# DMA transposes of attention's exponentials issued one step sooner, the first output tile turned inside the last gate/up unit, and two value banks exchanged

## The chip, the core and the metric

The kernel runs on one core of one Trainium2 chip. The metric is the device time of one execution in microseconds; lower is better. The core's engines work side by side, each through its own queue in order: TensorE (PE, with its weight loads PEld), VectorE (DVE), ScalarE (ACT), GpSimd (POOL), and SyncE (SP), which in this kernel issues every DMA. Matmul results go to PSUM, here named as eight banks, `bank0` to `bank7`.

## The reference

A sequence of 2048 rows of width 576 goes through an attention with a memory over four segments and through a gated feed-forward block; a gate per row mixes the two.

```python
g = _sigmoid((x * gate_w).sum(-1, keepdims=True))
a = _A_ref(x, wq, wk, wv, wo, beta)      # 32 heads of 18, 4 segments of 512
b = (_silu(x @ w_gate) * (x @ w_up)) @ w_down   # 576 -> 4608 -> 576
return g * a + (1 - g) * b
```

Shortened: within a segment the mask adds -1e9 where the query's index is below the key's. For each segment

```python
logits = jnp.einsum("bhqd,bhkd->bhqk", qs, ks) * scale + mask
p = _softmax(logits, axis=-1)
a_dot = jnp.einsum("bhqk,bhkd->bhqd", p, vs)
num, den = phi(qs) @ M, phi(qs) @ z + 1e-6
outs.append(sig * (num / den) + (1.0 - sig) * a_dot)   # sig = sigmoid(beta) per head
M, z = M + phi(ks).T @ vs, z + phi(ks).sum()
```

and the outputs of all heads go through `wo`.

## The kernel before

Float32 accuracy is reached with pairs of rounded values: an operand is split into a high and a low part (ScalarE copies the high part, VectorE subtracts it: the helper `split`, lines 128 and 129), and three matmuls take the place of one.

**Phase one (0 to about 220 us): projections.** For each of four segments `qk` makes nine chains of queries and keys (14 matmuls of 512 columns each, line 151), and `v_step` makes eight steps of values and of the row gate (14 matmuls of 288 or 290 columns, same line). The chains of the first segment take the banks 0 to 4 in turn (`first_tile`), those of later segments 0, 1 and 2 (`chain_tile`). The steps of the values take the banks that the list in `v_tile` names, one after the other; its first eight entries are those of the first segment. A chain's bank is last read by VectorE in line 368 (`ph`), a value step's by line 388, or by line 390 for the steps of the second half, which hold the gate's column. In segments two to four, sums of keys and values (`upd_gen`) run in between in the banks 3 and 4 (`pair_tile`).

**Phase two (about 220 to 1650 us): feed-forward and attention interleaved.** There are 72 gate/up units (`seq`): two halves of the rows (`HALF`) by 36 column blocks. Each unit is seven products (`seven`, lines 998 and 1001) after Strassen's scheme, and each is followed by a `tick`, which calls `beat`: it first runs the functions that are due (a list `due`; `defer(k, fn)` puts fn at the k-th beat from now; `plan` holds offsets, to which one is added), then a down group or two, and then steps of attention, according to a credit. Every third unit, 16 down groups (`down_group`, line 851: 9 matmuls of 320 or 256 columns from three blocks `hs` and `ds`) are put into the list `groups`; line 856 adds their result into `ya`. At the end of each half the groups of the last three blocks are left; for the first half they run in a break of ten beats (`BREAK`), for the second in the output stage.

Attention is a generator, `att_gen`, whose steps `tau` run six to a unit `u` of two heads (64 units). Step t of a unit (t = 0 to 4) holds one bank of logits: `s_bank` (PE line 720, VectorE's row minimum line 726) at tau = t, `e_bank` (ScalarE's exponentials line 738, POOL's triangle line 746) one step later, `p_bank` three steps later (`PL`): VectorE rounds to float16 (line 752) and POOL makes the rest (line 753). `x_bank` (line 757) has SP transpose both halves by DMA into `pt`, `XL` steps after `s_bank`. It is the last thing that its step does. At the sixth step of the next unit `v_unit` (lines 768 and 769) multiplies the five transposed tiles of a unit with the values. `p` has 4 buffers, `pt` has 7. At tau = 1 to 3 of a unit SP also issues the loads of the next unit's `qst` and `kst` (line 804), in the sixth sometimes the values `v` (line 206). Between these, in the same queue of SP, stand the loads and stores of the units: `raw` (line 213), `rh` (246), `draw` (218), `dc` and `dw` (833, 838), `rr` and `rc` (241, 239), `wc` (705).

**Output stage (about 1650 to 1746 us).** When attention is done (`c_open`), the weights `wo` are loaded in six pieces and split (lines 888 to 892), and the first tiles of attention's result are loaded (`c_load`: `o` and the memory's part `me`, lines 897 and 901). `c_tr` adds the two on POOL (line 913), copies a piece (line 914), turns the tile on PE in five transposes (lines 917 and 919, into bank 5 or 6 and bank 7), and splits the result. The loop over n = 0 to 16 turns tile n, does `downs(k)` (k of the 16 groups that are left), then for tile n - 1 both column halves: 14 matmuls with `wo`, `downs(1)`, and the mixing on VectorE (lines 1129 and 1130).

Of the kernel before, what the change touches and what calls it, by code (L numbers as in the profile page):

```python
# [36 lines left out]
NB = 8 * NSEG  # L37
NST = 2
PL = 3
XL = 5  # L40
KEPT = 2
HALF = ((2, 3), (0, 1))
TICK = ((0.57, 1.0), (0.47, 1.0))
# [22 lines left out]
def gated_mix(ctx, tc, xT, xrest, wf, wfr, wfh, wd, wv, wo, beta, cmask, ident, bmask, out):  # L66
# [32 lines left out]
    def banks(*ids):  # L99
        turn = cycle(ids)  # L100
        return lambda shape=(P, L): ps.tile(list(shape), F32, name=f"bank{next(turn)}")
# [3 lines left out]
    pair_tile = banks(3, 4)  # L105
    first_tile = banks(0, 1, 2, 3, 4)
    lone_tile = banks(7)
    v_tile = banks(5, 6, 7, 3, 4, 5, 6, 7, *8 * (5, 6, 7))
    a_tile = banks(0)
    x_tile = banks(1)  # L110
    y_tile = banks(2)
# [15 lines left out]
    def split(hi, lo, src):  # L127
        nc.scalar.activation(hi, src, AF.Copy)  # L128
        nc.vector.tensor_sub(lo, src, f32(hi))  # L129
# [31 lines left out]
    def xs_split(xs, raw):  # L161
        nc.scalar.activation(xs, raw, AF.Copy)
        nc.vector.tensor_sub(xs[64:128], raw[64:128], f32(xs[64:128]))
# [40 lines left out]
    def v_fetch(k):  # L204
        VP[k] = ap.tile([P, 4, 8, 3, E], BF, name="v")
        nc.sync.dma_start(VP[k], vd[k // 4, k // 2 % 2][:, :, 8 * (k % 2):8 * (k % 2) + 8])
# [477 lines left out]
    with ExitStack() as st:  # L684
# [12 lines left out]
        def row_tile():  # L697
            return rw.tile([P, L], F32, name="row")
# [93 lines left out]
        def att_gen():  # L792
            N = 12 * NB

            def at(t):
                return 5 * (t // 6) + t % 6 if 0 <= t < N and t % 6 < 5 else None

            for tau in range(N + 10):
# [17 lines left out]
                if n == 5 and 1 <= u <= 2 * NB:  # L816
                    v_unit(u - 1)
                    if u % 4 == 1 and u // 4 + 1 < 4 * NSEG:
                        v_fetch(u // 4 + 1)
                z = at(tau - XL)  # L820
                if z is not None:
# [39 lines left out]
        wos, tiles = [], {}  # L861
# [49 lines left out]
        def c_tr(o, me):  # L911
            if me is not None:
                nc.gpsimd.tensor_add(o[:, 0:D], o[:, 0:D], me)
            nc.gpsimd.tensor_copy(o[:, 576:640], o[:, 512:576])
            ta = half_tile([P, 4, P])
            for k in range(4):
                nc.tensor.transpose(ta[:, k], o[:, P * k:P * k + P], idt)
            tb = lone_tile([P, P])
            nc.tensor.transpose(tb, o[:, 512:640], idt)
            oh = cps[0].tile([P, 4, P], F32R, name="oh")  # L920
            ol = cps[0].tile([P, 4, P], F32R, name="ol")
            os_ = cps[0].tile([P, P], F32R, name="os")
            split(oh, ol, ta)
            xs_split(os_, tb)
            r = []
            for k in range(4):
                r += [oh[:, k], ol[:, k], oh[:, k]]
            return r + [os_, os_]
# [30 lines left out]
        def feed(half, f):  # L959
            return [(f // CH, i, hf, hs, ds, yas[half], half) for i in range(8) for hf in range(2)]  # L960
# [32 lines left out]
        def seven(t, j, first=True):  # L993
# [6 lines left out]
                    n += 1  # L1000
            nc.tensor.matmul(t, rem[:, RPOS[j]], XR[j], start=False, stop=True, skip_group_check=True)  # L1001

        draw = {}
        for o, fn in start:
            defer(o - 7, fn)
        for pos, (half, f) in enumerate(seq):
            if f == 0:
                yas[half] = yp.tile([P, 8, D], F32, name="ya")
            q = f % CH
            nxt = seq[pos + 1] if pos + 1 < len(seq) else None  # L1010
            if q == 0 and f:
                groups += feed(half, f - 1)
            plan = []
            if nxt:
                plan += w_fetch(nxt[1]) if nxt[0] and nxt[1] < KEPT else w_make(*nxt)
                if nxt != (0, 1):
                    plan.append((1 if nxt[1] else 10, lambda f=nxt[1]: r_fetch(f)))
                for n, h in enumerate(BLOCKS.get(pos, ())):
                    plan += r_block(h, 4 * n)
                if f + 2 < FT:  # L1020
                    wraw_of[f + 2] = [None, None]
                    for u in range(2):
                        plan.append(((2, 5)[u] if f or not half else 5 + u, lambda u=u, f=f: wraw_of[f + 2].__setitem__(u, w_load(f + 2, u))))
            if pos == FT - 2:
                X2, XR2 = [[None, None] for _ in range(7)], [None] * 7
                plan += [(o + 8, fn) for o, fn in x_second(X2, XR2)]
            for o, fn in plan:
                defer(o + 1, fn)
            step = [0]

            def tick():
                k = step[0]
                step[0] += 1
                if k == 0:
                    while stores:
                        nc.sync.dma_start(*stores.pop(0))
                if half == 0:
                    if (q, k) in ((0, 3), (1, 3), (2, 2)):
                        draw[f] = d_load(f)
                    if (q, k) in ((1, 1), (1, 7), (2, 4)):  # L1040
                        g = f - 1 if k == 1 else f
                        ds[half, g] = d_split(g, draw.pop(g))
                elif (q, k) in ((1, 0), (1, 2), (2, 1)):
                    g = f - 1 if k == 0 else f
                    ds[half, g] = d_fetch(g)
                beat(k, half)

            ops, rem = wops.pop((half, f)), rhs[f % 2]
            hh = fp.tile([P, 2, L], F32R, name="hh")
            hl = fp.tile([P, 2, L], F32R, name="hl")  # L1050
            hs[half, f] = hh, hl
            a, y, xx = a_tile(), y_tile(), x_tile()
            p5, sg0, sg1 = (row_tile() for _ in range(3))
            seven(a, 0)
            nc.scalar.activation(xx, a, AF.Copy)  # L1055
            tick()
            seven(y, 1)
            nc.scalar.activation(p5, y, AF.Copy)
            tick()
            seven(a, 2, False)  # L1060
            y = y_tile()
            nc.vector.tensor_add(y, a, p5)
            tick()
            seven(xx, 3, False)
            nc.scalar.activation(sg0, xx, AF.Copy)  # L1065
            tick()
            seven(a, 4, False)
            xx = x_tile()
            nc.scalar.activation(xx, a, AF.Copy)  # L1069
            nc.vector.tensor_add(p5, a, p5)  # L1070
            tick()
            nc.scalar.activation(sg0, sg0, AF.Silu)  # L1072
            seven(y, 5, False)
            nc.scalar.activation(sg1, y, AF.Silu)
            exp_table()
            tick()
            tick()
            seven(xx, 6, False)
            nc.vector.tensor_mul(sg0, xx, sg0)
            nc.vector.tensor_mul(sg1, p5, sg1)  # L1080
            if q == CH - 1:
                defer(2, lambda t=(hh[:, 0], hl[:, 0], sg0): split(*t))
            else:
                split_by(2, hh[:, 0], hl[:, 0], sg0)
            split_by(3, hh[:, 1], hl[:, 1], sg1)
            tick()
            assert not groups
            if f == FT - 1:
                groups += feed(half, f)
                if half == 0:  # L1090
                    for n in range(BREAK):
                        beat(None if n > 1 else n)
                    XO, XR = X2, XR2
                    assert not groups
# [13 lines left out]
        def downs(k):  # L1108
            for _ in range(min(k, len(groups))):
                down_group(*groups.pop(0))  # L1110

        ffs = {n: f_load(n) for n in range(2)}
        for n in range(17):
            if n < 16:
                if n + 2 < 16:
                    tiles[n + 2] = c_load(n + 2)
                    ffs[n + 2] = f_load(n + 2)
                nxt = c_tr(*tiles.pop(n))
                downs(2 if n else 4)
            if n:  # L1120
                tt = order[n - 1]
                ff = ffs.pop(n - 1)
                for hf in range(2):
                    c = slice(288 * hf, 288 * hf + 288)
                    t = chain_tile()
                    products(t[:, :288], ops, w_mov(wos[hf], 288))
                    downs(1)
                    if hf == 0:
                        nc.vector.tensor_scalar_mul(ff, ff, g1[:, tt:tt + 1])
                    nc.vector.scalar_tensor_tensor(ff[:, c], t[:, :288], gg[:, tt:tt + 1], ff[:, c],  # L1130
                                                   op0=OP.mult, op1=OP.add)
                    if hf == 0 and sent:
                        nc.sync.dma_start(*sent.pop(0))
                    if n == 16:
                        nc.sync.dma_start(out[0, P * tt:P * tt + P, c], ff[:, c])
                if n < 16:
                    sent.append((out[0, P * tt:P * tt + P, :], ff))
            ops = nxt
# [54 lines left out]
```

## Time and profile before

| | us |
|---|---|
| three runs | 1742.91, 1745.12, 1744.81 |
| median | 1744.81 |
| the profiled execution | 1747.73 |
| its span, first to last instruction | 1746.0 |
| its mean granted clock of TensorE | 0.998 |

The profile is of one execution. Its page gives the busy time of each engine; a view by stage gives it for stretches of the span, where the numbers are: the stretch, its length, then for PE, PEld, DVE, ACT and POOL the busy time and in brackets the number of instructions, then the granted clock of TensorE (1.00 is full speed), the busy share of the DMA engines, and GB/s. The list of waits has, for who waited and whom for, the total, the number and the longest. A row of the timeline is: start, duration, engine, line, operation, output and inputs, shapes, the number of instructions that were merged, and in brackets the idle time of the engine before it and what ended it. Rows of SP (marked SPq) are issues of DMAs: their duration is that of the issue, not of the transfer. A row of the chain of waits is: start, duration, what.

### The profile page before, as it was taken

Reading aid. Unit: us, or ns where it says so; the run is one execution under the profiler, and the core shown is the slowest. Engines: PE = TensorE matmul, PEld = TensorE weight load, DVE = VectorE, ACT = ScalarE, POOL = GpSimd, SP = SyncE. Lnnn points to the kernel's source line nnn. Section 1 sums busy time; section 2 is a strip of 40 time slices with the busy share of each in tenths; the row PEclk is TensorE's granted clock in tenths of the full one; section 3 lists DMA queues with packets and bytes.
Section 4 is the critical chain, followed back from the end, with each engine's and each line's share of the span. In section 5 each row is a group of like instructions: output and inputs, shape, how many; then the busy total and the mean of one; then the engine's idle time right before and its main releaser. Section 6 shows DMA issues by size and latency. Waiting matters only on the chain.

```text
span 1746.0 us, 34931 instructions
## 1 busy us (share of the span) xinstructions
PE 1715.8 (98%) x11868; PEld 1483.9 (85%) x11868; DVE 1368.6 (78%) x3231; ACT 1093.6 (63%) x2198; POOL 936.3 (54%) x1194
## 2 busy tenths in 40 slices
PE   9999999999999999999999999999999999999999
PEld 7899978878888888887887788888888888888799
DVE  6567587989898889898989677787888777887655
ACT  7666575765676577667656755665666576656511
POOL 4434645656665656665666555555555555555221
PEclk9999999999999999999999999999999999999999
DMA  7654499998998888897979976777687668866544
GB/s 263 237 190 154 149 307 179 213 221 180 225 216 206 175 207 199 187 199 192 209 146 287 263 176 132 188 168 157 156 185 173 155 149 186 169 129 147 168 134 139
DMA packets 524003, 328.06 MB, mean 188 GB/s; under 512 B 411184, under 2 KB 460336, under 8 KB 523824
## 3 DMA queue, kind: packets, MB, share of 16 engines
q1 hardware_dynamic: 523824, 325.83, 76.6%
q8 instruction: 93, 1.52, 0.4%
q14 instruction: 86, 0.70, 0.1%
HBM read 165.76 MB, written 76.09 MB: 139 GB/s over the span
## 4 chain that ended last, share of the span: by engine, by line
PE 78%; ACT 8%; DVE 4%; DMA 3%; issue 3%; POOL 2%; SPq 1%; DVEq 0%; ACTq 0%; POOLq 0%
PE bank L998 29%; PE bank L851 25%; PE bank L151 10%; PE bank L1001 5%; PE bank L720 3%; PE bank L768 2%; ACT L1072 1%; PE bank L769 1%; ACT L991 1%; DMA pt<-p 1%; ACT pe L738 1%; PE bank L406 1%; POOL ws L256 1%; DVE hl L941 1%; PE bank L342 1%
## 5 line engine op out<-in xcount | busy, mean ns | idle before, releaser
L753 POOL TENSOR_TENSOR p<-pe,p 128x512 f16<-128x512 f32 x320 | 374.4, 1170 | 457.7 <-DVE p L752 438.2
L851 PE MATMUL bank<-dw,hh 128*128 128x320 f32 (+1 forms) x2304 | 491.2, 306 | 4.1 <-ACT hh L128 2.8
L851 PEld LDWEIGHTS bank<-dw,hh 128*128 128x128 f32 x2304 | 383.3, 191 | 15.6 <-ACT hh L128 3.1
L738 ACT ACTIVATE pe<-bank,mb 128x512 f32<-128x512 f32 (+3 forms) x512 | 246.2, 522 | 219.7 <-DVE mb L726 216.0
L851 PE MATMUL bank<-dw,hl 128*128 128x320 f32 (+1 forms) x1152 | 341.6, 297 | 0.2 <-DVE hl L129 0.2
L726 DVE CUSTOM_DVE_ANT_0 scr<-bank,cm 128x512 bf16<-128x512 f32 (+3 forms) x512 | 246.1, 481 | 7.4 <-PE bank L720 0.6
L851 PEld LDWEIGHTS bank<-dw,hl 128*128 128x128 f32 x1152 | 219.1, 190 | 0.4 <-DVE hl L129 0.4
L856 DVE TENSOR_TENSOR ya<-bank,ya 128x320 f32<-128x320 f32 x352 | 157.7, 452 | 78.7 <-PE bank L851 77.9
L1001 PE MATMUL bank<-xr,rh 128*128 128x512 f32 x504 | 196.3, 390 | 0.0
L746 POOL TENSOR_SCALAR_AFFINE_SELECT pe<-pe 128x256 f32<-128x256 f32 (+1 forms) x320 | 151.1, 473 | 31.2 <-ACT pe L738 21.6
L752 DVE CAST p<-pe 128x512 f16<-128x512 f32 x320 | 145.3, 454 | 2.3 <-DMA pt<-p 2.3
L256 POOL TENSOR_TENSOR ws<-raw 128x256 f32<-128x256 f32 x140 | 123.2, 880 | 15.8 <-DVE wo__22847 L263 4.1
L720 PE MATMUL bank<-kst,qst 108*128 108x512 bf16 (+3 forms) x512 | 125.4, 306 | 5.0 <-ACT pe L738 4.9
L1001 PEld LDWEIGHTS bank<-xr,rh 128*128 128x128 f32 x504 | 94.6, 188 | 20.5
L941 DVE TENSOR_TENSOR hl<-row,hh 128x512 fp32r<-128x512 f32 x120 | 101.4, 845 | 10.8 <-ACT hh L940 10.4
L1065 ACT ACTIVATE row<-bank 128x512 f32<-128x512 f32 x72 | 43.1, 598 | 93.6 <-PE bank L1001 93.5
L1070 DVE TENSOR_TENSOR row<-bank,row 128x512 f32<-128x512 f32 x72 | 49.6, 689 | 58.4 <-ACT bank L1069 58.2
L1072 ACT ACT_TABLE_LOAD x72 | 92.4, 1283 | 1.3
L991 ACT ACT_TABLE_LOAD x72 | 92.4, 1283 | 1.0
L768 PE MATMUL bank<-v,pt 128*128 128x57 bf16 x1280 | 77.0, 188 | 8.8 <-DMA pt<-p 5.7
L1055 ACT ACTIVATE bank<-bank 128x512 f32<-128x512 f32 x72 | 41.7, 579 | 67.0 <-PE bank L1001 66.9
L366 POOL TENSOR_TENSOR q<-qr,q 128x512 bf16<-128x512 f32 x36 | 44.5, 1235 | 72.7 <-ACT q L365 61.9
(2166 smaller groups left out, 4139.0 us busy)
## 6 DMA issues: line engine op xcount, KB each, us to landing
raw<-in_wf_dram SPq DMA_DIRECT2D x140, 256.0 KB
rh<-rc SPq DMA_DIRECT2D x72, 336.0 KB
dc<-dw SPq DMA_DIRECT2D x36, 576.0 KB
dw<-dc SPq DMA_DIRECT2D x36, 576.0 KB
stk<-q SPq DMA_DIRECT2D x32, 384.0 KB
draw<-in_wd_dram SPq DMA_DIRECT2D x36, 288.0 KB
rc<-rt SPq DMA_DIRECT2D x42, 224.0 KB
vd<-vps SPq DMA_DIRECT2D x8, 912.0 KB
```

What stands on the lines that cost most here:

```text
L151: nc.tensor.matmul(t, st[n], mv[n], start=(n == 0), stop=(n == 13))
L256: (nc.gpsimd.tensor_sub if sub else nc.gpsimd.tensor_add)(src[j], p(), q())
L720: nc.tensor.matmul(t[:, c:c + w], qs[:KR, pr, P * i:P * i + P], ks[:KR, pr, 0:w], start=True, stop=True)
L726: nc.vector.tensor_tensor_reduce(scr[:, :w], t[:, c:c + w], cm[:, L - w:L], -SCALE, 3.0e38, OP.add, OP.min, m[:, k:k + 1])
L738: nc.scalar.activation(pe[:, c:c + w], t[:, c:c + w], AF.Exp, bias=m[:, k:k + 1], scale=SCALE)
L746: nc.gpsimd.affine_select(d, d, pattern=pat, compare_op=OP.is_ge, fill=0.0, base=0, channel_multiplier=1)
L752: nc.vector.tensor_copy(p[:, 0], pe)
L753: nc.gpsimd.tensor_sub(p[:, 1], pe, p[:, 0])
L851: nc.tensor.matmul(t, p, q[:, cs], start=(n == 0), stop=(n == 3 * CH - 1))
L856: nc.vector.tensor_add(ya[:, i, cs], t, ya[:, i, cs])
L998: nc.tensor.matmul(t, w[:, p, z], x[z][:, q], start=first and n == 0, stop=False, skip_group_check=True)
L1001: nc.tensor.matmul(t, rem[:, RPOS[j]], XR[j], start=False, stop=True, skip_group_check=True)
```

## The change

Three things are changed. `XL` goes from 5 to 4, so that `x_bank` runs one step of attention sooner, at the end of the step before. In `v_tile`, the entries for the steps 3 and 4 of the first segment become the banks 4 and 0 (they were 3 and 4). And tile 0 of the output stage is turned (`c_tr`) in the last gate/up unit, at the fourth beat, between its fourth and fifth product; the loop takes it from the list `early`, and the down groups are dealt out otherwise: none for n = 0 (four before), none ahead of tile 0's products for n = 1 (two before), two from n = 2 on as before.

```diff
@@ -37,7 +37,7 @@
 PL = 3
-XL = 5
+XL = 4
@@ -105,7 +105,7 @@
-    v_tile = banks(5, 6, 7, 3, 4, 5, 6, 7, *8 * (5, 6, 7))
+    v_tile = banks(5, 6, 7, 4, 0, 5, 6, 7, *8 * (5, 6, 7))
@@ -1000,6 +1000,7 @@
+        early = []
         draw = {}
         for o, fn in start:
             defer(o - 7, fn)
@@ -1011,6 +1012,8 @@
             plan = []
+            if not nxt:
+                plan.append((3, lambda: early.append(c_tr(*tiles.pop(0)))))
             if nxt:
@@ -1115,8 +1118,8 @@
-                nxt = c_tr(*tiles.pop(n))
-                downs(2 if n else 4)
+                nxt = c_tr(*tiles.pop(n)) if n else early.pop()
+                downs(2 if n > 1 else 0)
             if n:
```

## The prediction

> **What bounds the kernel now.** The page and its table by stage come first: which engine has no room.
>
> ```profile
> PE 1715.8 (98%) x11868; PEld 1483.9 (85%) x11868; DVE 1368.6 (78%) x3231; ACT 1093.6 (63%) x2198; POOL 936.3 (54%) x1194
> ...
> 250.00:300.00 50.00, 46.52 (x338) 39.95 (x336) 39.78 (x96) 30.92 (x64) 29.18 (x41) 1.00 0.89 198
> 1650.00:1700.00 50.00, 46.78 (x344) 45.96 (x343) 27.20 (x53) 9.17 (x21) 12.37 (x15) 0.97 0.48 161
> ```
>
> TensorE is busy 1715.8 of 1746.0 us, so only some 30 us are open to any reordering. Of these 3.5 us are lost in 250 to 300 and 3.2 in 1650 to 1700, there with a clock below 1. The change adds and removes no matmul, so what it can give is a share of these waits. The list of waits names them:
>
> ```profile
> PE bank L768 <- DMA pt<-p: 5.7, 4, 2.2
> PE bank L720 <- ACT pe L738: 4.9, 7, 1.0
> PE bank L851 <- ACT hh L128: 2.8, 1, 2.8
> ```
>
> The first belongs to the transposes, the third to the output stage. Each part is now priced at its place.
>
> **Transposes one step sooner (XL).** The four waits for `pt`, on the timeline of PE, three by their rows, are
>
> ```profile
> 297.23 0.20 PE L768 MATMUL bank<-v,pt 128*128 128x57 bf16 x1 [1.75 <-DMA pt<-p]
> 359.00 0.20 PE L768 MATMUL bank<-v,pt 128*128 128x57 bf16 x1 [1.31 <-DMA pt<-p]
> 936.85 0.20 PE L768 MATMUL bank<-v,pt 128*128 128x57 bf16 x1 [2.21 <-DMA pt<-p]
> ```
>
> and the fourth is what 5.7 leaves: 5.7 - 5.27 = 0.4. All lie in the first half or at its end. Why the data is late there is read from the queue of SyncE (SP) and from POOL, which makes the second half of `p`:
>
> ```profile
> 287.57 1.16 POOL L753 TENSOR_TENSOR p<-pe,p 128x512 f16<-128x512 f32 x1 [2.78 <-DVE p L752]
> ...
> 275.35 1.30 SPq L239 DMA_DIRECT2D rc<-rt  x2
> 280.21 0.37 SPq L241 DMA_DIRECT2D rr<-in_wfh_dram  x1
> 281.29 4.61 SPq L757 DMA_TRANSPOSE pt<-p  x2
> ...
> 291.58 1.37 SPq L757 DMA_TRANSPOSE pt<-p  x1
> 293.00 0.98 SPq L804 DMA_DIRECT2D kst<-stk  x2
> 294.09 1.23 SPq L757 DMA_TRANSPOSE pt<-p  x1
> ```
>
> The transpose at 294.09 is the last of its unit and the one that PE waits for at 297.23. Counting back through the five subtractions of its unit, its `p` was finished by the POOL row at 287.57 + 1.16 = 288.73: it stood 5.4 us ready behind SP's own queue. With XL = 4 each transpose is issued at the end of the step before, about where the one ahead of it stood. The last one thus jumps the two `kst` loads (293.00 to 294.09, 1.1 us). The first of the unit (281.29) goes in front of the `rr` load, before which SP sat idle from 275.35 + 1.30 = 276.65 to 280.21; one transpose costs SP about 1.3 us, and this one is now paid out of that idle time, so that all later ones move up by 1.3 more. Together 2.4 us: more than the 1.75 that PE waits, and `p` allows 5.4. The unit of 359.00 shows the same queue:
>
> ```profile
> 353.17 0.90 SPq L804 DMA_DIRECT2D kst<-stk  x2
> 354.18 1.23 SPq L757 DMA_TRANSPOSE pt<-p  x1
> ```
>
> 1.0 us from the pair of loads, and 1.3 if its first transpose finds idle time too, make 2.3 against a wait of 1.31. I take both waits and the 0.4 as gone: 1.75 + 1.31 + 0.4 = 3.5 us. From below, if only the jump over two loads counts, 1.1 + 1.0 + 0.4 = 2.5; from above all 5.7.
>
> The 2.21 at 936.85 I take as nothing, because another wait stands right behind it:
>
> ```profile
> 936.50 0.61 ACT L128 ACTIVATE hh<-row 128x512 fp32r<-128x512 f32 x1
> 937.15 0.69 DVE L129 TENSOR_TENSOR hl<-row,hh 128x512 fp32r<-128x512 f32 x1 [1.23 <-ACT hh L128]
> 943.27 1.21 DVE L856 TENSOR_TENSOR ya<-bank,ya 128x320 f32<-128x320 f32 x3
> 943.80 0.51 PE L851 MATMUL bank<-dw,hh 128*128 128x256 f32 x2 [1.02 <-DVE ya L856]
> ```
>
> This is the break between the halves. PE's next work after the value matmuls is the down groups, whose last factor needs `hh` (ready 937.11) and `hl` (937.84), and after three groups a bank that VectorE frees at 943.27. Neither depends on `pt`. PE arrives 2.2 us sooner and stands until 943.80 all the same. Bounds: 1.0 gained (the second wait shrinks with a quieter DVE) to 1.7 lost (a longer stand halves the clock, as below).
>
> What is pushed back: SP's order is a queue, so every load that a transpose passes goes 1.24 to 1.37 us later: the `qst`/`kst` loads of the next unit, the weight loads `raw`, the rests `rh`, the stores `dc` and `rc`. In half two (960 to 1620) SP itself waits at the transposes:
>
> ```profile
> SPq L757 <- POOL pe L746: 115.4, 55, 5.5
> ```
>
> There POOL sets their time, so they gain nothing, and SP stands earlier in front of them with the loads of a step behind it, 115.4 / 55 = 2.1 us at a time. The cover is the distance to the use: the tightest place I found is in the rival below (5.6 us). I price it at nothing; without cover it is 0.44 us a unit there. `p` has 4 buffers and is read sooner, `pt` has 7 of which 6 are live at most: no new wait.
>
> **Two banks of the first segment's values.** The value step 3 took bank 3, which the last projection chain had just filled; it takes bank 4 now, and step 4 takes bank 0.
>
> ```profile
> 42.98 0.68 DVE L368 SCALAR_TENSOR_TENSOR ph<-bank,ph 128x512 f32<-128x512 f32 x1
> 43.72 1.85 PE L151 MATMUL bank<-vw,xo 128*128 128x288 f32 x12 [1.26 <-DVE ph L368]
> ...
> 52.22 0.14 DVE L390 COPY gl<-bank 128x1 f32<-128x1 f32 x1
> ...
> 53.22 0.62 PE L151 MATMUL bank<-xo,qhi 128*128 128x512 f32 x2
> ```
>
> Step 3's wait of 1.26 us goes, since bank 4's chain was read four chains ago. But bank 0 is the bank of the next segment's first chain (53.22), and its last reader is now step 4's copy of the gate column, which ends at 52.36 (ScalarE and VectorE set its pace, not PE). The chain would come at 53.22 - 1.26 = 51.96 and starts at about 52.4: 0.8 us gained, 0.4 given back. Bounds: 0 and 1.26.
>
> **First output tile turned in the last gate/up unit.** Before, PE transposes tile 0 after the last unit and then wants four down groups at once, whose third factor is not split yet:
>
> ```profile
> 1650.02 0.54 PE L851 MATMUL bank<-dw,hh 128*128 128x320 f32 x2
> ...
> 1653.94 0.56 PE L851 MATMUL bank<-dw,hh 128*128 128x320 f32 x2 [2.80 <-ACT hh L128]
> ...
> 1660.24 0.60 PE L917 MATMUL bank<-idt,o 128*128 128x128 f32 x4
> ...
> 1660.95 2.40 PE bank L851 x18
> ...
> 1653.27 0.61 ACT L128 ACTIVATE hh<-row 128x512 fp32r<-128x512 f32 x1
> 1654.53 0.65 DVE L892 TENSOR_TENSOR wo<-raw,wo 128x480 fp32r<-128x480 f32 x1
> 1649.48 1.44 POOL L913 TENSOR_TENSOR o<-o,me 128x576 f32<-128x576 f32 x1 [8.20 <-DMA me<-med]
> 1650.98 0.58 POOL L914 COPY o<-o 128x64 f32<-128x64 f32 x1
> ...
> 1651.50:1654.91 3.41, 0.80 (x3) 0.55 (x4) 1.65 (x3) 2.96 (x8) 0.06 (x1) 1.00 1.07 391
> 1654.91:1658.32 3.41, 3.15 (x14) 2.86 (x14) 2.58 (x6) 0.14 (x1) 1.65 (x2) 0.50 0.43 161
> ```
>
> Two groups take 2.40 us at full clock (the chain's row, 18 matmuls), four take 4.80. From 1650.02 to 1660.24 are 10.22, so 5.4 us are lost: the wait of 2.80, small ones, and 3.41 us at the granted clock of 0.50, which follow a stretch in which PE was busy 0.80 of 3.41 (half of 3.41 is 1.7). [...]
>
> Now tile 0 is turned between the fourth and fifth product of the last unit. Its data is there (tile 0's add precedes tile 1's, which only waits for its `me`), and PE pays the same for a turn wherever it stands (at most 0.7 us, 1660.24 to the next group in the chain's row at 1660.95), so it is through with unit and turn at 1650.02 as before. Then it turns tile 1: POOL ends that tile's add at 1650.92 and its copy at 1651.56, after which one transpose is left, to 1651.8. Of these 1.8 us 0.7 are work: a new wait of 1.1 us. Then come 14 matmuls of tile 0's first product, with all its inputs split, up to about 1653.7; then a group, whose `hh` (1653.88) and `hl` (0.7 later) arrive while it does its six matmuls of the two earlier blocks (0.9 us); then the second product, whose last weight piece is split at 1655.18, about 0.3 us late. New waits 1.4, gain 5.4 - 1.4 = 4.0 us. PE is busy over half of that time, so I expect no halved clock. Behind the waiting transposes nothing else on PE can go; on ScalarE and VectorE the two splits of tile 0 move ahead into idle time. Bounds: 5.4 (no new wait) and 0 (the second tile's `me` lands 4 us later).
>
> **Sum.** 3.5 + 0 + 0.8 + 4.0 = 8.3 us. The profiled execution took 1747.73 us with a span of 1746.0 and 1.7 around it: it becomes 1739.4. It lies 2.9 above the median of the runs (1744.81); against that, 1736.5. Adding the bounds: 2.5 - 1.7 + 0 + 0 = 0.8 gained at the worst, 3.5 + 1.0 + 1.26 + 5.4 = 11.2 at the best.
>
> **Rivals.** (1) The transposes' gain is given back: PE comes sooner to work that VectorE has not released, as at 943.80. For: DVE is busy 39.78 of 50 us in 250 to 300. Against: PE's other waits there are under 1.1 us. Left are 0.8 + 4.0: 1740.0. (2) The tail's wait only changes its name: tile 1's `me` or the last weight piece is later than before and PE stands for `o` as long as it stood for `hh`. For: tile 1's add had waited 8.20 us for its load. Against: that load had landed at 1649.48, and nothing in front of it moves. Left are 4.3: 1740.5. (3) Slower: SP's loads come too late. The place is the first half, where SP has least room:
>
> ```profile
> 832.44 0.89 SPq L804 DMA_DIRECT2D kst<-stk  x2
> 833.44 1.24 SPq L757 DMA_TRANSPOSE pt<-p  x1
> ...
> 838.96 0.39 PE L720 MATMUL bank<-kst,qst 108*128 108x512 bf16 x1
> ```
>
> The loads end issue at 833.33 and are used at 838.96, 5.6 us later. The slowest landing above, from issue to PE, is 359.00 - 354.18 = 4.8; 0.8 is left, and the transpose that now passes costs 1.24, so PE would wait 0.44. In all 32 units of the half that is 14 us: 1744.8 - 8.3 + 14 = 1750.5. From 8.3 / 32 = 0.26 us a unit on it is slower. For: DMAs do land slowly there (share 0.89). Against: no wait of L720 for a load stands in the list, only 4.9 us for ScalarE's bank. (4) The transposes don't move in effect, because POOL is late for them: true in half two, false for the rows above; it ends near rival 1.
>
> **Chances.** Forecast 0.60 (own range 1734 to 1740), rivals 1 and 4 together 0.14, rival 2 0.10, rival 3 0.16. A measurement tells 0.2%, 3.5 us, from no change: faster means below 1741.3. The forecast lies below; of rivals 1, 4 and 2, half or somewhat more (0.14 of 0.24); so faster 0.74, same 0.10, slower 0.16. The range 1732 to 1745 holds the forecast with the best bound (1744.8 - 11.2 = 1733.6 and a little run-to-run), rivals 1, 2 and 4, and leaves rival 3 out.
>
> **What will show it.** Right: the waits of L768 for `pt` at about 297, 359 and 467 are gone, the one at the break is replaced by a wait for `hh` or L856; no wait for L368 near 43; no `hh` wait at the end, a wait for `o` of about 1 us instead, and no stretch with clock 0.50 there. Wrong: L720 or a PE weight load waits for `kst`, or POOL's L256 for `raw`; the gate/up units of half one grow longer; a new halved clock at the break.

## The result, and the profile after

| | before | changed |
|---|---|---|
| median of six runs, us | 1744.33 | 1738.11 |
| lowest to highest | 1742.30 to 1745.69 | 1737.18 to 1739.56 |
| profiled execution, us | 1747.73 | 1738.29 |
| its span | 1746.0 | 1736.6 |

The ratio is 0.9962, with a 95% interval of 0.9952 to 0.9972: the change gains 6.2 us by the medians. The two profiled executions lie 9.4 us apart, because the profiled execution of before is longer than all 82 others of it on record (the longest of these took 1747.27). 1.8 us of the difference are there at the first projection matmul, ahead of every changed instruction.

The rows of the changed kernel that answer to those of before: first the page's busy times,

```profile
PE 1714.6 (99%) x11868; PEld 1482.5 (85%) x11868; DVE 1370.0 (79%) x3231; ACT 1094.1 (63%) x2198; POOL 935.1 (54%) x1194
```

then two stretches of the table by stage,

```profile
250.00:300.00 50.00, 48.84 (x350) 42.14 (x349) 42.40 (x103) 31.16 (x65) 31.30 (x44) 1.00 0.95 196
...
1650.00:1700.00 50.00, 50.00 (x386) 50.00 (x385) 27.28 (x57) 5.36 (x14) 11.53 (x16) 1.00 0.43 145
```

and the list of TensorE's waits (in all, times, longest).

```profile
PE bank L720 <- ACT pe L738: 4.7, 6, 1.2
PE bank L768 <- ACT pe L738: 3.1, 2, 1.9
...
PE bank L917 <- POOL o L913: 1.1, 1, 1.1
...
PE bank L998 <- DMA wo__13458<-wc: 0.3, 1, 0.3
```

Span less busy time, PE's idle time went from 1746.0 - 1715.8 = 30.2 to 22.0 us; the other 1.2 of the 9.4 lie in its busy time. L768 no longer waits for `pt` at all. The stretch from 250 to 300 gained 2.3 busy microseconds, and the one from 1650 to 1700, which had 46.78 and a clock of 0.97, is full at clock 1.00. New in these rows are the wait for `o` and a small one for a weight `wo` that came late by DMA.

SP's timeline in the unit that had waited at 297.23:

```profile
272.17 2.30 SPq L757 DMA_TRANSPOSE pt<-p  x1
276.75 0.37 SPq L241 DMA_DIRECT2D rr<-in_wfh_dram  x1
...
285.54 1.27 SPq L757 DMA_TRANSPOSE pt<-p  x1
...
288.33 1.23 SPq L757 DMA_TRANSPOSE pt<-p  x1
289.60 1.02 SPq L804 DMA_DIRECT2D kst<-stk  x2
```

The two `kst` loads that stood before the last transpose (293.00, then 294.09) now stand behind it, and the unit's first transpose (272.17) fills idle time ahead of the `rr` load. The `kst` loads come 3.4 us sooner than before and the last transpose 5.76, which is 2.4 more, the two parts that the forecast had added. PE's own first matmul of this unit's values, before and now:

```profile
294.47 0.20 PE L768 MATMUL bank<-v,pt 128*128 128x57 bf16 x1
```

```profile
290.63 0.20 PE L768 MATMUL bank<-v,pt 128*128 128x57 bf16 x1
```

PE is there 3.84 us sooner, so against PE the transpose gains 5.76 - 3.84 = 1.9 us, hardly more than the 1.75 that PE had waited. PE's timeline at the break between the halves:

```profile
931.07 0.56 PE L851 MATMUL bank<-dw,hh 128*128 128x320 f32 x2 [1.35 <-ACT hh L128]
...
937.71 0.50 PE L851 MATMUL bank<-dw,hh 128*128 128x256 f32 x2 [1.34 <-DVE ya L856]
```

The wait of 2.21 for `pt` is gone, and a new one for `hh` and a longer one for `ya` stand in its place. The matmul that ends the second started at 943.80 before, 6.09 us later; the last wait of L998 ahead of the break ended at 928.26 before and at 922.16 now, 6.10 apart. Nothing was gained between them. This stretch, from that wait of L998 to the end of the last wait for `ya`, is 15.53 to 15.56 us long in all thirteen profiles with XL of 5 or 4, whether PE waits 0 or 2.21 us for `pt` in it.

The output stage, on PE's and then on POOL's timeline:

```profile
1645.78 0.66 PE L917 MATMUL bank<-idt,o 128*128 128x128 f32 x4 [1.09 <-POOL o L913]
```

```profile
1644.26 1.47 POOL L913 TENSOR_TENSOR o<-o,me 128x576 f32<-128x576 f32 x1 [8.24 <-DMA me<-med]
```

The wait of 2.80 for `hh` and the halved clock behind it have gone. The turn of tile 1 waits 1.09 us for the sum on POOL, which ends at 1645.73.

### The profile page after: what moved, and what is told of

The parts are those of the page before. It is cut to its first block, busy times and chain, and to the rows that moved or that the text cites. A ratio compares the mean times of both kernels' runs of the same rounds, so it can differ in the third digit from the quotient of the medians.

```text
span 1736.6 us, 34910 instructions
## 1 busy us (share of the span) xinstructions
PE 1714.6 (99%) x11868; PEld 1482.5 (85%) x11868; DVE 1370.0 (79%) x3231; ACT 1094.1 (63%) x2198; POOL 935.1 (54%) x1194
## 3 DMA queue, kind: packets, MB, share of 16 engines
q8 instruction: 93, 1.52, 0.4%
## 4 chain that ended last, share of the span: by engine, by line
PE 81%; ACT 9%; DVE 4%; DMA 2%; issue 2%; POOL 1%; SPq 1%; DVEq 0%; ACTq 0%; POOLq 0%
PE bank L998 30%; PE bank L851 26%; PE bank L151 10%; PE bank L1001 5%; PE bank L720 4%; PE bank L768 2%; ACT L1075 1%; PE bank L769 1%; ACT L991 1%; ACT pe L738 1%; PE bank L406 1%; PE bank L452 1%; ACT row L1075 1%; PE bank L342 1%; DVE hl L941 1%
## 5 line engine op out<-in xcount | busy, mean ns | idle before, releaser
L256 POOL TENSOR_TENSOR ws<-raw 128x256 f32<-128x256 f32 x140 | 123.6, 883 | 18.3 <-DMA raw<-in_wf_dram 7.2
L720 PE MATMUL bank<-kst,qst 108*128 108x512 bf16 (+3 forms) x512 | 125.4, 306 | 4.7 <-ACT pe L738 4.7
L941 DVE TENSOR_TENSOR hl<-row,hh 128x512 fp32r<-128x512 f32 x120 | 101.6, 847 | 10.9 <-ACT hh L940 10.6
L151 PE MATMUL bank<-xo,qhi 128*128 128x512 f32 x264 | 83.1, 396 | 0.1
L256 POOL TENSOR_TENSOR ws<-raw,ws 128x256 f32<-128x256 f32 x70 | 56.6, 808 | 48.4 <-DVE wo__22573 L263 10.9
```

The lines of the kernel that those rows point to most:

```text
L151: nc.tensor.matmul(t, st[n], mv[n], start=(n == 0), stop=(n == 13))
L256: (nc.gpsimd.tensor_sub if sub else nc.gpsimd.tensor_add)(src[j], p(), q())
L720: nc.tensor.matmul(t[:, c:c + w], qs[:KR, pr, P * i:P * i + P], ks[:KR, pr, 0:w], start=True, stop=True)
```

## The experiments

Each kernel was timed beside before on the same chip, in three groups, in which before has the medians 1744.6, 1743.86 and 1745.09. Gains are worked out from the ratios; the differences of the medians lie up to 0.8 us from them.

**Transposes alone.**

```diff
-XL = 5
+XL = 4
```

> The kernel before with the transposes one step sooner and nothing else. My theory (the five waits of the value products for pt go away, the half break stays as it was): the gain between units 3 and 16 is 3.5 us by the forecast and 4.6 by the trace of the changed kernel, so 1739.7 to 1740.8 beside 1744.3, a ratio of 0.9974 to 0.9980; the waits of L768 for pt are gone from the trace, and the tail still has the 2.80 us wait for hh and the halved clock behind it. Rival (later loads on SP cost what the transposes give): 1743.5 to 1745, with new waits of L768, L720 or L998 for DMAs that add up to 3 us or more. Rival (most of the gain was the tail's): within 0.1% of before.

Measured: 1742.07 against 1744.6, ratio 0.9985 (0.9976 to 0.9994), a gain of 2.6 us where 3.5 to 4.6 was expected. The waits for `pt` (four in the profile of before) are all gone, as expected. Part of the price is in PE's timeline:

```profile
967.62 1.63 PE L998 MATMUL bank<-xo,wo__13458 128*128 128x512 f32 x6 [0.99 <-DMA wo__13458<-wc]
...
1647.81 0.56 PE L851 MATMUL bank<-dw,hh 128*128 128x320 f32 x2 [1.79 <-ACT hh L128]
```

A weight that SP loads behind the transposes comes 0.99 us late. The tail still stands for `hh`.

**Banks alone.**

```diff
-    v_tile = banks(5, 6, 7, 3, 4, 5, 6, 7, *8 * (5, 6, 7))
+    v_tile = banks(5, 6, 7, 4, 0, 5, 6, 7, *8 * (5, 6, 7))
```

> The kernel before with the banks of value steps 3 and 4 changed (3,4 to 4,0) and nothing else. My theory: the wait of 1.26 us at 43.72 goes and the x split, a little later, takes back most of it, so 0.5 us net at the end of segment two's first chain and 1743.8 beside 1744.3: a ratio of 0.9997, not to be told from 1 by times alone, but the trace has no wait near 40.5 to 44 and one of 0.3 to 0.6 us for xs near 54. Rival by the forecast's term: 0.8 us, 1743.5, with the wait for xs absent and one for bank 0 in its place. Rival: the earlier start is lost altogether further on, ratio 1.0000 and the first unit at the same time as before.

Measured: 1744.04 against 1744.6, ratio 1.0001 (0.9992 to 1.0010): by times nothing. In the trace the wait near 41 to 44 is gone and this one, on PE's timeline, has come:

```profile
53.27 0.50 PE L151 MATMUL bank<-xs,qhi 128*128 128x512 f32 x1 [0.54 <-DVE xs L163]
```

The six kernels with the old banks (before and five of these experiments) wait 0.45 to 1.26 us at L151 for `ph`, 0.9 in the mean; the eight with another bank for step 3 wait 0.27 to 0.63 for `xs`, 0.5 in the mean. The net is 0.4 us, too small for the times.

**Tail alone** (early turn and new deal of the down products).

```diff
+                plan.append((3, lambda: early.append(c_tr(*tiles.pop(0)))))
-                nxt = c_tr(*tiles.pop(n))
-                downs(2 if n else 4)
+                nxt = c_tr(*tiles.pop(n)) if n else early.pop()
+                downs(2 if n > 1 else 0)
```

> The kernel before with the early turn of the first output tile and the new deal of the down products, and nothing else. My theory: 4.0 us by the forecast, 4.4 by the changed kernel's trace, of which 5.4 are the removed wait for hh (2.80) and the half clock behind it, and 1.1 come back as the wait of the second tile's turn for o: 1739.9 to 1740.3, a ratio of 0.9975 to 0.9977. Rival (the wait only changes its name, the clock is halved all the same): 0 to 1 us, 1743.3 to 1744.3, with a wait of over 2 us and a half-clock stretch after 1640. Rival (the weight piece is late): a wait of L1069 or L1072 for a DMA of 1 us or more.

Measured: 1742.62 against 1744.6, ratio 0.9989 (0.9980 to 0.9998), 1.9 us. The trace has what was expected: from 1640 on PE waits 0.18 and 0.17 us, and no stretch there has a lower clock until the very end. The time gives half of what the trace gives; more on this below.

**Early turn alone**, with the down products dealt four and two as before.

```diff
+                plan.append((3, lambda: early.append(c_tr(*tiles.pop(0)))))
-                nxt = c_tr(*tiles.pop(n))
+                nxt = c_tr(*tiles.pop(n)) if n else early.pop()
```

> The kernel before with the early turn alone; the down products are dealt as before (four behind the first turn's place, two behind the second's), so the four that cover the wait for hh are moved by the missing turn only. Theory A (it is the dealing that hides the wait): TensorE still waits for hh, now up to 0.6 us longer since the four transposes of the turn no longer stand in front of it, the clock is halved behind it, and the gain in the tail is under 1 us: 1743.5 to 1745. Theory B (the early turn is what takes VectorE's and ScalarE's work off the tail, the dealing is of no weight): the wait for hh is under 0.5 us and the tail is 3 to 4 us shorter, 1740.3 to 1741.3.

Measured: 1746.3 against 1744.6, ratio 1.0005 (0.9996 to 1.0014): no gain, if anything a loss. PE's timeline has the wait for `hh` as theory A has it:

```profile
1651.21 0.55 PE L851 MATMUL bank<-dw,hh 128*128 128x320 f32 x2 [2.69 <-ACT hh L128]
```

**The deal alone**, with tile 0 turned in its old place.

```diff
-                downs(2 if n else 4)
+                downs(2 if n > 1 else 0)
```

> The kernel before with the down products dealt as in the changed kernel (none behind the first two turns' places) but the first tile turned in its old place behind the last unit. My theory (both edits are needed: the products of the first tile need its split, which stands behind hh on ACT): TensorE waits 2 us or more for oh, ol or os at L151 in place of hh at L851, a half-clock stretch follows, and the time is within 1.5 us of before, 1743 to 1745.5. Rival (the deal alone is what gains): waits in the tail under 1 us, 3 to 4 us under before.

Measured: 1748.08 against 1745.09, ratio 1.0015 (1.0006 to 1.0024): 2.6 us slower, more than expected, and the wait is at another place. The timelines of PE, ACT and DVE, in this order:

```profile
1655.25 0.45 PE L919 MATMUL bank<-idt,o 128*128 128x128 f32 x1 [5.50 <-DVE os L163]
...
1652.71 0.57 ACT L128 ACTIVATE oh<-bank 128x512 fp32r<-128x512 f32 x1
...
1654.81 0.29 DVE L163 TENSOR_TENSOR os<-bank,os 64x128 fp32r<-64x128 f32 x1
```

The fifth transpose of tile 1 needs the bank that tile 0's fifth transpose has filled, and this bank is free only when DVE has made `os`, which stands behind the splits of `hh` and of the weight pieces. PE stands 5.50 us. So neither edit of the tail gains alone: the early turn brings tile 0's splits ahead of this work, and the deal uses that.

**One step further.**

```diff
-XL = 4
+XL = 3
```

> The changed kernel with the transposes sooner by one further step (XL 3 in place of 4). My theory: no wait of L768 for pt is left to be removed, and POOL's pe decides when a transpose can start, so SP's queue stands behind L757 longer (over 160 us in the two halves' later part) and its loads come later; the time is 1738.1 to 1741, with new waits of PE for DMAs (wo__13458 by L998, qst or kst by L720) of 0.3 us up to 2. Rival (the sooner the better): 1736 to 1737.5, the remaining waits of L768 for pe of 1.9 and 1.2 us gone as well. Rival (SP blocked for long): 1745 or more, loads late by over 5 us.

Measured: 1777.55 against 1743.86, ratio 1.0191 (1.0176 to 1.0206): 33 us slower, on the side of the rival that had SP blocked, and far more than any of the expectations had put a number to. The list of waits has SP and then two engines that need its loads:

```profile
SPq L757 <- POOL pe L746: 314.1, 138, 7.1
SPq L757 <- POOL ws L256: 215.8, 98, 7.8
SPq L757 <- POOL p L753: 69.5, 40, 4.7
...
POOL ws L256 <- DMA raw<-in_wf_dram: 27.8, 10, 4.4
...
ACT dw L940 <- DMA draw<-in_wd_dram: 18.3, 11, 2.9
```

In front of the transposes SP stands 599 us here by the first three rows. The same rows for the changed kernel are

```profile
SPq L757 <- POOL pe L746: 267.8, 134, 5.9
SPq L757 <- POOL ws L256: 125.6, 81, 6.2
SPq L757 <- POOL p L753: 39.2, 33, 2.7
...
POOL ws L256 <- DMA raw<-in_wf_dram: 7.2, 3, 3.5
```

433 us together, against 294 before:

```profile
SPq L757 <- POOL pe L746: 161.0, 94, 5.5
SPq L757 <- POOL ws L256: 96.0, 73, 6.1
...
SPq L757 <- POOL p L753: 37.3, 34, 3.3
```

A transpose waits in SP's queue for POOL's half of `p`, and every load behind it waits too. (A transpose reads only `p`; the other rows name the POOL operation whose event came last.) With XL = 4 this shows on POOL: L256 waits 6.3 to 10.6 us for `raw` in the six profiles, against 0 to 5.4 in the six with XL = 5 and the old order of loads, and it reaches PE as the late `wo`. With XL = 3 it reaches ACT. How it comes to PE is read in one place, on the timelines of SP, ACT and PE:

```profile
634.24 1.24 SPq L757 DMA_TRANSPOSE pt<-p  x1
635.58 0.52 SPq L218 DMA_DIRECT2D draw<-in_wd_dram  x1
...
638.45 0.69 ACT L940 ACTIVATE dw<-draw 128x576 fp32r<-128x576 f32 x1 [0.88 <-DMA draw<-in_wd_dram]
...
645.80 0.38 PE L720 MATMUL bank<-kst,qst 108*128 108x512 bf16 x1 [1.95 <-ACT pe L738]
```

The load of `draw` is issued behind the transpose, ACT waits 0.88 us for it, has no free time from there to its exponentials, and PE waits for a bank that these free. PE's idle time, span less busy time on the page, is 1776.8 - 1726.5 = 50.3 us, 28 more than in the changed kernel. The other 12 us of the 40 between the two spans lie in PE's busy time; two more stretches of halved clock (from 200 to 300 and from 600 to 700 the mean clock is 0.98, 1.00 in the changed kernel) account for an estimated 3.4 of them, and the rest wasn't split up.

**Loads behind the transposes** of the same step, before's XL of 5.

```diff
-                if 1 <= n <= 3 and u + 1 < 2 * NB:
-                    for d in stack_loads(u + 1)[3 * n - 3:3 * n]:
-                        nc.sync.dma_start(*d)
...
                     x_bank(z)
+                if 1 <= n <= 3 and u + 1 < 2 * NB:
+                    for d in stack_loads(u + 1)[3 * n - 3:3 * n]:
+                        nc.sync.dma_start(*d)
```

> The kernel before, with the transposes in their old step, but the two or three loads of qst and kst of each step issued by SP behind that step's transposes and x loads. My theory (a step's shift gains by what the last transposes no longer stand behind on SP: two loads of 1.0 to 1.1 us): the waits of L768 for pt shrink, 1.75 at 297 to about 0.7 and 1.31 at 359 to about 0.3, and the time is 1742 to 1743. Rival (POOL's pe, or the transposes' own 1.2 us each, sets when they land): the waits stay within 0.2 us and so does the time, 1744 to 1745. Rival (the loads are then late for L720): new waits for qst or kst and 1745 or more.

Measured: 1744.68 against 1743.86, ratio 1.0006 (0.9997 to 1.0016): nothing gained. The waits in the trace did shrink, from 2.7 to 5.7 us in the six other kernels with XL = 5 to 2.0: those at 359 (the tail alone has none there either) and 467 are gone, while the first, expected at 0.7, stays at

```profile
292.74 0.20 PE L768 MATMUL bank<-v,pt 128*128 128x57 bf16 x1 [1.19 <-DMA pt<-p]
```

This is below the 1.75 of before, but above the 0.79 to 0.98 of the five others. So the jump over two loads can be part of the mechanism, but it is not all, and by times it gained nothing here. The trace has a wait of 1.66 us of L720 for `pe` at 628 (0.99 before) and one of 3.27 for `hh` in the tail (2.80 before); whether these belong to the edit isn't settled.

**Value step 4 in bank 3.**

```diff
-    v_tile = banks(5, 6, 7, 4, 0, 5, 6, 7, *8 * (5, 6, 7))
+    v_tile = banks(5, 6, 7, 4, 3, 5, 6, 7, *8 * (5, 6, 7))
```

> The changed kernel with value step 4 of segment one in bank 3 in place of bank 0. Theory A (bank 0's last reader at L390 holds back segment two): the start of segment two's first chain comes 0.27 us or more sooner than 50.20 against the products before it, and the gain stays: 1737.6 to 1737.9. Theory B (the split of x on DVE and ACT paces segment two): the wait of L151 for xs grows from 0.50 by as much as the chain starts sooner, and the time is that of the changed kernel, ratio to it 1.000.

Measured: 1737.76, ratio to before 0.9967 (0.9954 to 0.9980), no different from the changed kernel. On PE's timeline the first chain of segment two starts without a wait, and then

```profile
53.05 0.50 PE L151 MATMUL bank<-xs,qhi 128*128 128x512 f32 x1 [0.63 <-DVE xs L163]
```

The wait for `xs` is 0.63 where the changed kernel has 0.55 behind a wait of 0.10 at the start of the chain: the sum is the same, as theory B has it. (In the changed kernel's second profile `xs` costs 0.52 and the start nothing.)

**The changed kernel again.**

> The changed kernel, unaltered. My theory: the place of the half-clock stretches other than the one at the half break is a matter of phase: the 1.88 us wait of L768 for pe in unit 31 may or may not have a halved clock of 3.41 us behind it, which moves the time by up to 1.7 us; the one at 931.88 stands where the two waits for hh and ya lie, in each profile. The first 1.78 us that the changed kernel had won before its first altered instruction vary by as much. Rival: both are caused by the change, and then the halved stretch near 809 and the start agree with the first profile within 0.2 us.

Measured: 1738.52 against 1743.86, ratio 0.9969 (0.9956 to 0.9981). In this profile unit 31 has the same wait for `pe`, 1.90 us, and no halved clock. The tables by stage of the first profile and of this one, each with the row that holds the wait and the one behind it:

```profile
805.59:809.00 3.41, 1.53 (x36) 1.15 (x36) 1.98 (x6) 3.41 (x10) 0.48 (x1) 1.00 0.87 225
809.00:812.41 3.41, 3.41 (x21) 2.77 (x18) 2.05 (x5) 1.45 (x4) 3.41 (x5) 0.50 0.47 84
```

```profile
803.78:807.19 3.41, 1.59 (x7) 1.03 (x6) 1.63 (x5) 3.40 (x10) 0.00 (x0) 1.00 1.00 263
807.19:810.60 3.41, 3.33 (x51) 3.02 (x51) 3.26 (x10) 2.37 (x7) 2.96 (x4) 1.00 0.28 77
```

So this stretch is no property of the change: before, with 1.88 us of wait, had none in its profile. Where it falls it costs an estimated 1.7 us, half of its 3.41. The start is not the change's doing either: all other profiles, with and without the edits, are 1.3 to 2.6 us ahead of the profile of before at the first projection.

**Transposes and banks without the tail; tail and banks without the transposes.** Each is the changed kernel with one part undone.

```diff
-                plan.append((3, lambda: early.append(c_tr(*tiles.pop(0)))))
-                nxt = c_tr(*tiles.pop(n)) if n else early.pop()
-                downs(2 if n > 1 else 0)
+                nxt = c_tr(*tiles.pop(n))
+                downs(2 if n else 4)
```

```diff
-XL = 4
+XL = 5
```

> The changed kernel with the tail as it was before (no early turn, four and two down products dealt), so transposes sooner and banks alone. If the parts add up: 2.2 to 2.6 us under before, what the transposes alone gave by times, and in the trace no wait of L768 for pt and a tail with a wait of L851 for hh of 1.8 to 3.3 us and one or two half-clock stretches behind it, 4 to 6.7 us in all. Rival (the tail's gain in times, 2.4 us, is less than its 4 to 5 us in the traces because something else paid): more than 3.5 us under before here, since then the rest must carry the 5.4 to 6.2 of the whole.

> The changed kernel with the transposes in their old step, so tail and banks alone. If the parts add up: 2.4 to 4 us under before; the waits of L768 for pt are back, 1.1 to 3.5 us up to unit 16 and some 1.6 us at the half break near 931, and the tail's waits stay under 1.2 us with no half clock after 1640. Rival (the tail is nearly all of the change): within 1 us of the changed kernel, 1738.5 to 1739.5.

Measured against 1745.09: 1742.88 without the tail, ratio 0.9989 (0.9980 to 0.9997), and 1741.01 without the transposes, ratio 0.9980 (0.9971 to 0.9989): gains of 1.9 and 3.5 us. The parts add up within the noise: 1.9 + 3.5 = 5.4, beside 6.6 and 5.4 for the whole in its two measurements (ratios 0.9962 and 0.9969). The 1.9 lies a little under the 2.2 to 2.6 that was expected, within its interval. The three parts each alone make 2.6 - 0.2 + 1.9 = 4.3; with 1.6 us of uncertainty on each, this is no proof that they help one another.

**The second tile's load three steps earlier.**

```diff
-            defer(6, lambda: tiles.update({1: c_load(1)}))
+            defer(3, lambda: tiles.update({1: c_load(1)}))
```

> The changed kernel with the load of the second output tile three steps earlier. My theory: the wait of the second turn (L917) for o, 1.09 and 0.40 us in two profiles, goes away, since POOL's sum at L913 waited 8.24 us for the load of me; the time falls by 0.4 to 1.1 us, which by times can hardly be told from the changed kernel's, 1737.0 to 1738.0 beside 1744.3. Rival (POOL or ACT is the later one, or the earlier load delays the weight pieces on SP): the wait of L917 stays at 0.4 or more, or L151 of the first product waits for a weight piece, and the time is the changed kernel's or up to 1 us more.

Measured: 1738.61 against 1745.09, ratio 0.9967 (0.9954 to 0.9979). The turn of tile 1 starts without a wait, and POOL's sum for it is done 6 us ahead; on PE's and POOL's timelines:

```profile
1645.24 0.60 PE L917 MATMUL bank<-idt,o 128*128 128x128 f32 x4
```

```profile
1637.29 1.85 POOL L913 TENSOR_TENSOR o<-o,me 128x576 f32<-128x576 f32 x1
```

The mechanism is as expected. The missing wait alone would not show it, since three of the five profiles with both edits of the tail and the load in its old step have none either. A gain under 1 us can't be told by the times. None of these kernels is faster than the changed one beyond the noise.

The table puts the traces side by side, in us. "For pt" is the total of L768's waits for `pt`, "late wo" that of L998 for `wo__13458`, "tail" that of PE's waits from 1640 on, "half" the length of the stretch at clock 0.50 behind them (half of it counts as lost, an estimate).

| kernel | XL | for pt | late wo | tail | half |
|---|---|---|---|---|---|
| before | 5 | 5.7 | 0 | 3.2 | 3.4 |
| banks alone | 5 | 3.7 | 0 | 2.3 | 3.4 |
| early turn alone | 5 | 4.1 | 0 | 3.7 | 6.8 |
| deal alone | 5 | 4.3 | 0 | 5.5 | 6.8 |
| loads behind the transposes | 5 | 2.0 | 0 | 3.3 | 6.8 |
| tail alone | 5 | 2.7 | 0 | 0.4 | 0 |
| tail and banks | 5 | 3.3 | 0 | 0.5 | 0 |
| transposes alone | 4 | 0 | 1.0 | 3.0 | 6.8 |
| transposes and banks | 4 | 0 | 1.2 | 3.0 | 6.8 |
| changed | 4 | 0 | 0.3 | 1.1 | 0 |
| changed, again | 4 | 0 | 0 | 0.4 | 0 |
| changed, value step 4 in bank 3 | 4 | 0 | 0 | 0.2 | 0 |
| changed, tile 1 loaded earlier | 4 | 0 | 1.0 | 0.2 | 0 |
| one step further | 3 | 0 | 0, but 2.9 for two other weights | 0.5 | 0 |

## Why the prediction was right, and where its terms were off

The forecast was 1736.5 with a gain of 8.3 us; 1738.1 with a gain of 6.2 came out. The mechanism of each part was the predicted one, except in the banks. By traces the terms make 1.8 + 0 + 0.4 + 4.9 = 7.1 us, so that a tail above its term hides part of what the other two lack. The sizes:

**Transposes, 3.5 predicted, 2.6 measured by times alone and 1.9 with the banks.** "I take both waits and the 0.4 as gone" was right: no kernel with XL = 4 has any of them. Two sizes were off. The 3.46 was read from a single profile that happened to stand highest: without the wait at the break (2.21 before, 1.04 to 1.64 in the five others), the six profiles with XL = 5 and the old order of loads wait 1.1 to 3.5 us for `pt` up to unit 16, 2.4 in the mean. And "What is pushed back ... I price it at nothing" was wrong by the late `wo`, 0.6 us in the mean of the six profiles with XL = 4 and absent from all with XL = 5. 2.4 - 0.6 = 1.8, near the times. Both parts of the predicted 2.4, the jump past two loads and the first transpose in idle time, are seen on SP. The run with the loads behind the transposes shows that the jump alone does not make the gain; the other part was not run alone.

**The break, nothing predicted, nothing measured.** PE stands for `hh` (1.35) and `ya` there as soon as `pt` is in time, and the stretch is as long in every profile (15.53 to 15.56 us), as forecast. The second wait is 1.0 to 1.4 in some profiles and 2.9 in others, at both XL. It was short where the halved clock came ahead of it and slowed PE on the way (1.34 until 935.29, halved from 930.07, in the second profile of the changed kernel), and long where it came behind (2.86 until 935.99, halved from 936.37, in the transposes alone).

**Banks, 0.8 predicted, 0.4 by traces, -0.2 (plus or minus 1.6) by times.** The failing step is the one that named bank 0's last reader as what limits the chain afterwards. The wait at the start of that chain is 0.10 in the changed kernel and 0 to 0.18 in the seven profiles with bank 0. What gives the gain back is the split of `x` for segment two, `xs`, 0.5 us: moving step 4 off bank 0 lets the chain start at once, and PE waits the longer for `xs`.

**Tail, 4.0 predicted; 4.9 by traces, 1.9 to 4.7 by times.** Before, and in the three experiments that leave the tail's code and the order of loads as they were, the waits and half of the halved stretch make 4.9, 4.0, 6.4 and 6.4 us, 5.4 in the mean; the five profiles with both edits, XL of 5 or 4 and the load in its old step leave 0.2 to 1.1, 0.5 in the mean: 5.4 - 0.5 = 4.9. The forecast's new waits of 1.4 were too high: tile 1's `o` costs 1.09 or 0.40 or nothing from profile to profile, and the 0.3 for the last weight piece never came. By times the part is worth 1.9 (tail alone), 3.5 (with the banks) and 3.5 or 4.7 (the whole's 5.4 or 6.6 less the 1.9 of its version without the tail's edits). Why the tail alone gives less than the traces is not settled. The mean clock of the executions rises from 0.9975 (33 of before) to 0.9982 (11 of the tail alone), which is 0.0006 of 1744 or 1.1 us, where the profiles with the old tail lose 1.7 or 3.4 us to the halved clock in it. So the executions without a profile may lose less there than the profiled ones did. This is not shown: the transposes alone, with the old tail, have 0.9981.

The forecast's 5.4 us in the tail count 1.7 of halved clock as regained, and they were: none of the seven profiles with both edits of the tail has such a stretch there. Of the rivals, the first and the fourth, by which the transposes bring nothing, do not fit the run of the transposes alone (1.0 to 4.2 us gained by its interval) and its missing waits. The second (the wait changes its name) fell with the wait for `o` of 1.09 or less. The third, SP's loads late, was no fantasy: it costs 0.6 us with XL = 4, and it is the one cause found for the 33 us with XL = 3, of which only the way shown above was followed to PE. Its place was wrong, though: not `kst` for L720, but `wo`, `raw` and `draw`.

## What to carry to other kernels

A queue that issues waiting transfers and loads in one order can have a steep optimum: here one step sooner removed all the waits for the transposes, the next one cost 33 us, because each transfer that waits at the queue's head holds the loads behind it. The list of the queue's own waits showed it coming (294, 433, 599 us) while TensorE's list still looked better. And a wait that is read from one profile has a spread of its own: here 1.1 to 3.5 us in six kernels with the same transposes, so a sum built on one trace should carry that spread in its range.

## What the runs showed of the hardware

The traces of before and of the changed kernel have two halved stretches each inside the kernel, and each lasts 3.413 us at a granted clock of 0.50. Their starts lie 716.79 us apart before (938.12 and 1654.91) and 122.88 in the changed kernel (809.00 and 931.88), which is 210 and 36 times that length.

In the halved stretch of the changed kernel's second profile, from 930.07, a round of three matmuls of 320 columns takes 0.80 us (931.20 to 932.00), and behind it 0.44 (936.46 to 936.90). So the half of a stretch that is counted as lost here is an estimate near what was measured: 0.36 of 0.80 is 0.45.

In unit 31 the work around the wait is the same in the profiles with XL of 5 or 4. In six of them PE was busy 1.52 to 1.55 of the 3.41 us that hold most of the wait, and the clock of the 3.41 behind was 0.50. In six others, the second profile of the changed kernel (shown above) among them, PE was busy 1.59 to 2.11, and the clock behind was 1.00. A wait of 1.9 us thus cost 1.9 in the one case and an estimated 3.6 (1.9 and half of 3.41) in the other. The busy time alone does not tell which: at the break 3.41 us with 1.89 busy, filled by matmuls of the down groups and the waits for `hh`, were followed by 3.41 at clock 0.50 (second profile of the changed kernel). There PE was busy 0.55 of the time, more than the half on which the forecast expected no halved clock in the tail:

```profile
926.66:930.07 3.41, 1.89 (x12) 1.37 (x11) 2.15 (x7) 3.18 (x6) 0.32 (x1) 1.00 1.04 310
930.07:933.48 3.41, 3.41 (x16) 3.33 (x14) 3.18 (x6) 2.40 (x5) 3.41 (x4) 0.50 1.03 398
```

Why the clock was 1.00 behind 1.59 busy in unit 31 and 0.50 behind 1.89 here stays open.
